# One pair of matmuls moved between two tiles, a one-column read for an order, and one more superblock of partial DMA sums

## The chip, the cores and the metric

The kernel runs on one core of one Trainium2 chip. The metric is the device time of one execution in microseconds. A core has a matmul engine (TensorE, "PE" in the profile, with its weight loads as "PEld"), a vector engine (VectorE, "DVE"), an activation engine (ScalarE, "ACT"), a general engine (GpSimd, "POOL") and a queue engine (SyncE, "SP"). Each works through its own list of instructions in order. They wait for one another by semaphores. Transfers are issued from the SP and POOL lists and land later.

## What is computed

Two operators in a row: a convolution of seven taps whose weights are a softmax that differs for each token and head, and a two-layer network with `h - tanh(h)` between the layers.

```python
def _attn_ref(x, weight_gen):          # x (8, 4096, 192), weight_gen (8, 4096, 8, 7)
    w = np.exp(weight_gen - max)  ;  w = w / (sum(w) + 1e-09)      # over the 7 taps
    x_pad = six rows of zeros ahead of each sequence
    out[b, s, h, g] = sum_k w[b, s, h, k] * x_pad[b, s + k, h, g]  # 8 heads of 24

def _moe_ref(x, w_in, w_out):          # x (32768, 192), w_in (192, 2048), w_out (2048, 192)
    h = x @ w_in
    g = h - np.tanh(h)
    return g @ w_out
```

## The kernel before, in words

**Superblocks.** The 32768 tokens are cut into 32 superblocks of 1024 tokens (`NTOT = 32`), eight tokens per partition. Superblock n goes through four stages, and the loop at L509 runs these stages of different superblocks side by side:

1. *Softmax weights* (ScalarE exp at L145, VectorE sums, reciprocals, scaling at L159 to L198), three superblocks ahead.
2. *Products* (`products`, L204): GpSimd multiplies the seven shifted views of x by their weights, one instruction per tap at L223, into bf16 tiles: taps 0, 2, 4 into `even`, taps 1, 3, 5 into `odd`, tap 6 into `last`. It runs two superblocks ahead. Then the taps must be added up. A DMA issued from GpSimd's list (L240) adds `odd` onto `even`. For superblocks in `PART` (2 to 5) it is issued after tap 3 and adds only the first two pairs of taps; for later ones it is issued after tap 5 and adds nearly all of the three pairs.
3. *Convolution sums* (`conv_sums`, L259): TensorE adds up what is left of the taps and turns the result around by matmuls with an identity, at L276, into PSUM tiles `pc`. A superblock in `PART` has five terms for each of the three channel chunks. A later one has four terms for chunks 0 and 1, five for chunk 2. The sums for superblock n + 1 stand in superblock n's part of TensorE's list: those of chunks 0 and 1 between the matmuls of output block 6 (the first six of its f steps are free of them), then those of chunk 2. Chunks 0 and 1 are copied out by ScalarE (L302), chunk 2 by VectorE (L300), into `convT`.
4. *The network* (`gemm1` L314, `gemm2` L340). The 2048 hidden units are 16 f tiles of 128. `gemm1(n, f)` is six matmuls of 64 rows by 512 columns into a PSUM tile `ph` (L319), then Tanh on ScalarE (`th`, L330), then `ph - th` on VectorE (`gt`, L331). `gemm2(i)` makes the output block i of 128 tokens; there are eight per superblock, each with sixteen f steps (L353). Superblock n's loop makes the blocks of superblock n - 1: after each two f tiles of `gemm1` comes one output block (`out_block`, L506, p = 0 to 7).

**Row halves.** The array is used as two halves of 64 rows that run at the same time: r = 0 and r = 1. In `gemm1` both halves add into the same result. In `gemm2`, half 0 does the first 64 hidden units of each f tile for block i, while half 1 does the other 64 for block i - 1. So a block is finished one `out_block` later, and then ScalarE copies it from its PSUM bank (`obank`, two of them, L372) to `out_sb`. The first matmul of block i writes the bank that block i - 2 has left, so it waits for that copy. For the very first block the second half could overtake the first half in the same bank, since the first has no partner yet. An order written out by hand (L363) makes the second half's first matmul wait for a ScalarE instruction that itself waits for the matmuls before: `g1_act[0]`, the Tanh of the last f tile but one.

**Buffers that matter here.** `ph` and `pc` share three PSUM buffers. So `gemm1(n, 1)` takes the buffer that f tile 14 of superblock n - 1 used, and waits for VectorE's subtraction of that tile. `gt` of each f tile has two buffers.

**The end of a superblock** (L547 to L573): f tiles 12 and 13, block 6 mixed with the convolution sums of chunks 0 and 1, chunk 2, the first two f steps of block 7, f tiles 14 and 15, and the other fourteen f steps of block 7. Then superblock n + 1 begins with f tiles 0 and 1 and its block 0.

The order of instructions is as written in the program (`tc.manual_schedule()`); semaphores are put in by the framework.

Of the kernel before, what the change touches and what calls it, by code (L numbers as in the profile page):

```python
# [8 lines left out]
FP32 = mybir.dt.float32  # L9
BF16 = mybir.dt.bfloat16  # L10

ACT = mybir.ActivationFunctionType
# [4 lines left out]
def kernel(  # L17
# [8 lines left out]
    nc = tc.nc  # L26
# [5 lines left out]
    P = nc.NUM_PARTITIONS  # L32
# [12 lines left out]
    NPAIR = K // 2  # L45
    ACC = NPAIR * J * D - J * R
    PLAIN = (0, 1)
    PART = (2, 3, 4, 5)
    assert S % TOK == 0 and D % R == 0 and H * GC == R and F % P == 0
    assert NFT == 2 * J, "one token block of the second matmul per pair of f tiles"  # L50

    const = ctx.enter_context(tc.tile_pool(name="const", bufs=1))
# [13 lines left out]
    obank = [psum_o.tile([P, 512], FP32, name=f"obank{i}", tag=f"obank{i}") for i in range(2)]  # L66
    zero = const.tile([1, D], FP32, name="zero")
    nc.vector.memzero(zero[:])

    x_of = {}  # L70
    wg_of = {}
# [5 lines left out]
    conv_of = {}  # L77
    g_of = {}
    last_act = {}
    g1_act = {}  # L80
    last_sub = {}
    last_exp = {}
    last_conv = {}
# [2 lines left out]
    def order(inst, other, reason):  # L86
        tc.add_manual_dep(
            inst.ins,
            other.ins.name,
            mybir.DependencyInfo(mybir.DependencyClass.Sync, mybir.DependencyReason.DATA),  # L90
            reason=reason,
        )

    def load_wg(n):
        b, s = divmod(n, NSB)
        s0 = s * TOK
        wg_t = wgpool.tile([P, J, H, K], FP32, name="wg_t")
        nc.sync.dma_start(  # L98
            out=wg_t[:],
            in_=weight_gen[b, s0 : s0 + TOK].rearrange("(p j) h k -> p j h k", p=P),  # L100
        )
        wg_of[n] = wg_t
# [39 lines left out]
    def softmax_exp(n):  # L142
        wg_t = wg_of.pop(n)
        e_t = wgpool.tile([P, J, H, K], FP32, name="e_t")
        last_exp[0] = nc.scalar.activation(  # L145
            out=e_t[:].rearrange("p j h k -> p (j h k)"),
            in_=wg_t[:].rearrange("p j h k -> p (j h k)"),
            func=ACT.Exp,
        )
        e_of[n] = e_t  # L150

    def softmax_tile():
        return wgpool.tile([P, J, H, K], FP32, name="wsm")

    def softmax_sum(n, j0=0, j1=J):

        if j0 == 0:
            zsum_of[n] = wgpool.tile([P, J * H], FP32, name="zsum")
        nc.vector.reduce_sum(  # L159
            out=zsum_of[n][:, j0 * H : j1 * H],  # L160
            in_=e_of[n][:, j0:j1].rearrange("p j h k -> p (j h) k"),
            axis=AX.X,
        )

    def softmax_recip(n, j0=0, j1=J):
        if j0 == 0:
            zr_of[n] = wgpool.tile([P, J * H], FP32, name="zr")
        nc.vector.reciprocal(zr_of[n][:, j0 * H : j1 * H], zsum_of[n][:, j0 * H : j1 * H])  # L168
# [35 lines left out]
    def products(n, taps=None, sums=None, hooks={}, behind=None):  # L204
# [16 lines left out]
        for eng, k, j0, j1 in taps or [(nc.gpsimd, k, 0, J) for k in range(K)]:  # L221
# [12 lines left out]
            if j1 == 1:  # L234
                first_halo[0] = mul
            if (k, n in PART) in ((3, True), (K - 2, False)) and n not in PLAIN:


                acc = 2 * J * D if n in PART else ACC
                nc.gpsimd.dma_start(  # L240
# [8 lines left out]
        if n in PLAIN:  # L249
            prods_of[n] = [[dst[k] for k in (sums or range(K))]] * NC  # L250
        elif n in PART:
            prods_of[n] = [[dst[4], even[:, 0], even[:, 1], dst[5], last[:]]] * NC
# [61 lines left out]
    def gemm1(n, f):  # L314
        convT = conv_of[n]
        ph = psum_h.tile([P, 2, HT], FP32, name="ph", tag="ph")
        for c in range(NC):
            for r in range(2):
                nc.tensor.matmul(  # L319
                    ph[:, r, :],  # L320
                    lhsT=w_in[r * R : (r + 1) * R, c, f * P : (f + 1) * P],
                    rhs=convT[r * R : (r + 1) * R, c, :],
                    start=(c == 0),
                    stop=(c == NC - 1),
                )
        th = tpool.tile([P, TOK], FP32, name="th")
        ph_f = ph[:].rearrange("p r t -> p (r t)")
        g1_act[0] = last_act.get(0)
        gt = gpool.tile([P, TOK], BF16, name=f"gt{f}", tag=f"gt{f}")
        last_act[0] = nc.scalar.activation(out=th[:], in_=ph_f, func=ACT.Tanh)  # L330
        last_sub[0] = nc.vector.tensor_sub(gt[:], ph_f, th[:])  # L331
        g_of.setdefault(n, []).append(gt)

    LAST = (NTOT - 1) * J
    LEAD = 5
    LATE = (1, 2, 3, 4, 5, 6)
    half = {}
    out_of = {}

    def gemm2(i, f0=0, f1=NFT, between=lambda f: None):  # L340

        ops = []
        for r, blk in ((0, i), (1, i - 1)):
            if not 0 <= blk < LAST:
                continue
            n, j = divmod(blk, J)
            if r == 0 and f0 == 0:
                half[blk] = obank[blk % 2]
            ops.append((r, n, j, half[blk]))
        for f in range(f0, f1):  # L350
            for r, n, j, po in ops:
                col = (j % 2) * HT + (j // 2) * P
                mm = nc.tensor.matmul(  # L353
                    po[:, 0:D],
                    lhsT=g_of[n][f][r * R : (r + 1) * R, col : col + P],
                    rhs=w_out[r * R : (r + 1) * R, f, :],
                    start=(r == 0 and f == 0),
                    stop=(r == 1 and f == NFT - 1),
                )
                if r == 1 and f == 0 and i in (1, LAST):  # L360


                    order(mm, g1_act[0] if i == 1 else last_act[0], "row tiles in one bank")  # L363
            between(f)
        if i > 0 and f1 == NFT:
            blk = i - 1
            n, j = divmod(blk, J)
            po = half.pop(blk)
            if j == 0:
                out_of[n] = opool.tile([P, J, D], FP32, name="out_sb")  # L370
            out_sb = out_of[n]
            last_act[0] = nc.scalar.activation(out=out_sb[:, j, :], in_=po[:, 0:D], func=ACT.Copy)  # L372
            if j == J - 1:
                out_of.pop(n)
                g_of.pop(n)
                nc.sync.dma_start(
                    out=out[n * TOK : (n + 1) * TOK, :].rearrange("(p j) e -> p j e", p=P),
                    in_=out_sb[:],
                )
# [126 lines left out]
    def out_block(n, p, f0=0, f1=NFT, between=lambda f: None):  # L506
        gemm2((n - 1) * J + p, f0, f1, between)

    for n in range(1, NTOT):  # L509
        for p in range(J):  # L510
            more = n < NTOT - 1
            if more and p == 6:
                break
            gemm1(n, 2 * p)
            gemm1(n, 2 * p + 1)
            if n == 1:

                if p == 0:
                    load_wg(5)
                if p <= 1:  # L520
                    softmax_sum(3, p * JH, (p + 1) * JH)
                elif p <= 3:
                    softmax_recip(3, (p - 2) * JH, (p - 1) * JH)
                else:
                    softmax_sum(4, (p - 4) * JH, (p - 3) * JH)
                if p == 2:
                    softmax_exp(4)
                if p == 3:
                    wsm_of[3] = (softmax_tile(), None, e_of[3], zr_of[3])
                    products(3)  # L530
            elif n + 3 < NTOT:
                if p == 0:
                    softmax_exp(n + 3)
                if p == 0 and n + 4 < NTOT:
                    load_wg(n + 4)
                if 1 <= p <= 2:
                    softmax_sum(n + 3, (p - 1) * JH, p * JH)
                if 3 <= p <= 4:
                    softmax_recip(n + 3, (p - 3) * JH, (p - 2) * JH)
            out_block(n, p)  # L540
            if p == 0 and 1 < n < NTOT - 2:
                products(n + 2, behind=last_sub[0])
            if p == 0 and n + 3 < NTOT and n not in LATE:
                load_x(n + 3)
        if not more:
            continue
        gemm1(n, 12)  # L547
        gemm1(n, 13)
        if n == 1:
            softmax_recip(4)  # L550

        pcs = []
        sums = conv_sums(n + 1, ((0, 1),), pcs)
        mix = -(-len(prods_of[n + 1][0]) * 2 * 2 * JH // (NFT - LEAD))
        out_block(n, 6, between=lambda f: some(sums, mix if f >= LEAD else 0))
        some(sums, K * 4 * JH)
        conv_out(n + 1, ((0, 1),), pcs)
        pcs = []
        some(conv_sums(n + 1, ((2,),), pcs), K * 4 * JH)


        out_block(n, 7, 0, 2)
        conv_out(n + 1, ((2,),), pcs, nc.vector)
        if n + 3 < NTOT:

            softmax_norm(n + 3, pcs[0][:, 0])
        gemm1(n, 14)
        gemm1(n, 15)
        out_block(n, 7, 2)
        if n in LATE:  # L570


            load_x(n + 3, last_conv[0])  # L573
# [36 lines left out]
```

## Time and profile before

The median of 13 executions is 757.44 us (756.44 to 758.04). The profiled execution took 758.04 us; its span from first to last instruction is 756.2 us.

| | us busy | share of the span | instructions |
|---|---|---|---|
| TensorE matmuls | 734.3 | 97% | 14784 |
| TensorE weight loads | 579.0 | 77% | 14784 |
| VectorE | 695.6 | 92% | 740 |
| ScalarE | 625.1 | 83% | 839 |
| GpSimd | 670.7 | 89% | 264 |

| group | count | mean ns of one |
|---|---|---|
| Tanh, 128x1024 (L330) | 512 | 1022 |
| subtraction, 128x1024 (L331) | 512 | 1219 |
| gemm2 matmul, 64x192 (L353) | 7936 | 243 |
| gemm1 matmul, 64x512 (L319) | 3072 | 378 |
| product of one tap (L223) | 218 | about 3070 |
| copy of an output block (L372) | 248 | 331 |
| accumulating DMA, 1024 KB (L240) | 26 | lands after 8800 |
| accumulating DMA, 768 KB (L240) | 4 | lands after 7600 |

A matmul's length in the profile reaches from its start to a modelled end. Matmuls overlap, so what one costs in a row of many is the distance between starts, and a sum of such rows can call TensorE busy while it waits for a moment. The same distance read between the two halves is a pair's. The granted clock of TensorE is full in all 40 slices of the profile.

### The profile page before, as it was taken

How to read it: one execution, taken by the hardware profiler on the slowest of the kernel's cores; microseconds unless marked ns; L12 is line 12 of the kernel's file. 1: busy time of each engine (PE TensorE's matmuls, PEld its weight loads, DVE VectorE, ACT ScalarE, POOL GpSimd, SP SyncE). 2: the span in 40 equal slices, each digit the busy share in tenths (PEclk: the TensorE clock that was granted, in tenths of full speed). 3: DMA queues.
4: the chain of work that ended last, by engine and by line, in shares of the span. 5: the costliest groups of instructions: out<-in, count | busy, mean ns of one | idle time of the engine just before them, and what ended most of it. 6: DMA issues, size and time to landing. Idle time of an engine off the chain costs nothing.

```text
span 756.2 us, 32326 instructions
## 1 busy us (share of the span) xinstructions
PE 734.3 (97%) x14784; PEld 579.0 (77%) x14784; DVE 695.6 (92%) x740; ACT 625.1 (83%) x839; POOL 670.7 (89%) x264
## 2 busy tenths in 40 slices
PE   3899999999999999999999999999999999999997
PEld 2477778877777877777877787778777777778777
DVE  7989999999999999999999999999999999998893
ACT  3888888788888888888888888888888888888883
POOL 7999999999999999999999999999999999999000
PEclk9999999999999999999999999999999999999999
DMA  8935544566546665554666544666544566542312
GB/s 225 212 80 164 158 149 101 129 184 177 158 138 170 185 183 142 139 139 143 181 186 170 115 132 150 175 180 187 112 130 148 170 185 172 120 113 63 79 45 86
DMA packets 25943, 111.08 MB, mean 147 GB/s; under 512 B 4703, under 2 KB 9551, under 8 KB 21838
## 3 DMA queue, kind: packets, MB, share of 16 engines
q1 hardware_dynamic: 14718, 77.03, 28.4%
q0 software_dynamic: 11088, 31.99, 24.8%
q8 instruction: 115, 1.88, 1.0%
q14 instruction: 22, 0.18, 0.1%
HBM read 54.52 MB, written 25.17 MB: 105 GB/s over the span
## 4 chain that ended last, share of the span: by engine, by line
PE 80%; POOL 17%; DMA 2%; issue 1%; SPq 0%; DVE 0%; ACT 0%; POOLq 0%
PE obank L353 37%; PE ph L319 36%; POOL even L223 7%; POOL odd L223 6%; PE pc L276 5%; POOL last L223 2%; PE po L390 1%; DMA even<-odd 1%; DMA x_t<-in_x_dram 1%; POOL wsm L198 0%; POOL even L240 0%; POOL w_in L432 0%; POOL w_out L419 0%; SPq L98 0%; DVE out_sb L404 0%
## 5 line engine op out<-in xcount | busy, mean ns | idle before, releaser
L331 DVE TENSOR_TENSOR gt<-ph,th 128x1024 bf16<-128x1024 f32 x512 | 602.5, 1219 | 36.0 <-ACT th L330 33.0
L330 ACT ACTIVATE th<-ph 128x1024 f32<-128x1024 f32 x512 | 497.3, 1022 | 72.4 <-PE ph L319 69.5
L353 PE MATMUL obank<-w_out,gt 64*128 64x192 bf16 x7936 | 407.9, 243 | 1.0 <-issue 0.5
L353 PEld LDWEIGHTS <-gt 64*128 64x128 bf16 x7936 | 355.4, 94 | 49.9 <-ACT th L330 0.8
L319 PE MATMUL ph<-convT,w_in 64*128 64x512 bf16 x3072 | 384.6, 378 | 4.7 <-DVE gt L331 2.7
L223 POOL TENSOR_TENSOR even<-x_t,wsm 128x1536 bf16<-128x1536 f32 x93 | 285.2, 3067 | 15.9 <-DVE gt L331 15.5
L223 POOL TENSOR_TENSOR odd<-x_t,wsm 128x1536 bf16<-128x1536 f32 x93 | 284.9, 3064 | 0.0
L319 PEld LDWEIGHTS <-w_in 64*128 64x128 bf16 x3072 | 177.3, 94 | 108.7 <-issue 20.1
L372 ACT ACTIVATE out_sb<-obank 128x192 f32<-128x192 f32 x248 | 82.0, 331 | 36.7 <-PE obank L353 30.0
L223 POOL TENSOR_TENSOR last<-x_t,wsm 128x1536 bf16<-128x1536 f32 x32 | 106.7, 3333 | 0.4 <-DMA x_t<-in_x_dram 0.4
L276 PE MATMUL pc<-ident,even 64*128 64x64 bf16 x2256 | 63.0, 191 | 1.3 <-DMA even<-odd 1.1
L276 PEld LDWEIGHTS <-even 64*128 64x128 bf16 x2304 | 59.9, 96 | 2.4 <-DMA even<-odd 1.2
L240 POOL DMA_DIRECT2D even<-odd x30 | 36.1, 1205 | 9.3 <-POOL odd L223 9.3
L276 PE MATMUL pc<-ident,last 64*128 64x64 bf16 x752 | 27.2, 191 | 9.5 <-POOL last L223 9.5
L302 ACT ACTIVATE convT<-pc 128x1024 bf16<-128x1024 f32 (+1 forms) x33 | 32.7, 993 | 2.4 <-PE pc L276 2.4
L276 PEld LDWEIGHTS <-last 64*128 64x128 bf16 x768 | 23.3, 96 | 9.7 <-POOL last L223 9.5
L159 DVE TENSOR_REDUCE zsum<-e_t 128x32 f32<-128x224 f32 (+1 forms) x61 | 23.7, 388 | 2.9 <-ACT e_t L145 2.9
L300 DVE CAST convT<-pc 128x512 bf16<-128x512 f32 x30 | 20.7, 690 | 4.5 <-PE pc L276 2.9
L145 ACT ACTIVATE e_t<-wg_t 128x448 f32<-128x448 f32 x32 | 18.5, 577 | 7.6 <-DMA wg_t<-in_weight_gen_dram 7.6
L168 DVE RECIPROCAL zr<-zsum 128x32 f32<-128x32 f32 (+1 forms) x58 | 20.3, 350 | 0.0
L198 DVE TENSOR_TENSOR wsm<-e_t,pc 128x448 f32<-128x448 f32 x28 | 17.4, 621 | 2.9
L276 PE MATMUL pc<-ident,odd 64*128 64x64 bf16 x400 | 14.4, 199 | 1.4 <-POOL odd L223 0.8
(28 smaller groups left out, 77.0 us busy)
## 6 DMA issues: line engine op xcount, KB each, us to landing
x_t<-in_x_dram SPq DMA_DIRECT2D x31, 1344.0 KB, 9.3
even<-odd POOLq DMA_DIRECT2D x26, 1024.0 KB, 8.8
out_dram<-out_sb SPq DMA_DIRECT2D x31, 768.0 KB, 7.2
wg_t<-in_weight_gen_dram SPq DMA_DIRECT2D x32, 224.0 KB, 9.7
even<-odd POOLq DMA_DIRECT2D x4, 768.0 KB, 7.6
x_t<-in_x_dram SPq DMA_DIRECT2D x1, 768.0 KB
w_out<-in_moe_w_out_dram POOLq DMA_DIRECT2D x1, 768.0 KB, 9.4
out_dram<-out_sb SPq DMA_DIRECT2D x4, 192.0 KB, 1.9
```

The costliest lines, as they stand in the source:

```text
L159: nc.vector.reduce_sum(out=zsum_of[n][:, j0 * H : j1 * H], in_=e_of[n][:, j0:j1].rearrange("p j h k -> p (j h) k"), axis=AX.X,)
L168: nc.vector.reciprocal(zr_of[n][:, j0 * H : j1 * H], zsum_of[n][:, j0 * H : j1 * H])
L223: mul = eng.tensor_mul(dst[k][:, :, j0:j1].rearrange("p c j h g -> p j h c g"), x_t[:, k + j0 : k + j1, :].rearrange("p j (h c g) -> p j h ...
L240: nc.gpsimd.dma_start(out=even[:].rearrange("p i c j h g -> p (i c j h g)")[:, 0:acc], in_=odd[:].rearrange("p i c j h g -> p (i c j h g)" ...
L276: nc.tensor.matmul(pc[r][:, col : col + R] if home else pc[:, r, col : col + R], lhsT=prods[c][gi][r * R : (r + 1) * R, c, 2 * j : 2 * j + ...
L300: eng.tensor_copy(out, pc[:, :, 0:cols].rearrange("p r (cj t) -> p r cj t", t=R))
L302: last_conv[0] = nc.scalar.activation(out=out, in_=pc[:, :, 0:cols].rearrange("p r (cj t) -> p r cj t", t=R), func=ACT.Copy,)
L319: nc.tensor.matmul(ph[:, r, :], lhsT=w_in[r * R : (r + 1) * R, c, f * P : (f + 1) * P], rhs=convT[r * R : (r + 1) * R, c, :], start=(c == ...
L330: last_act[0] = nc.scalar.activation(out=th[:], in_=ph_f, func=ACT.Tanh)
L331: last_sub[0] = nc.vector.tensor_sub(gt[:], ph_f, th[:])
L353: mm = nc.tensor.matmul(po[:, 0:D], lhsT=g_of[n][f][r * R : (r + 1) * R, col : col + P], rhs=w_out[r * R : (r + 1) * R, f, :], start=(r == ...
L372: last_act[0] = nc.scalar.activation(out=out_sb[:, j, :], in_=po[:, 0:D], func=ACT.Copy)
```

## The change

Three edits in one:

- In superblocks 2 to 31 the first f step of output block 0 (one matmul of each row half) is placed between f tiles 0 and 1 instead of behind f tile 1. The other fifteen f steps stay behind f tile 1. The name `FILL` stands for a 2 that was there before.
- In superblock 1, the second half of the first block waits for a new ScalarE instruction instead of the Tanh of f tile 2: a Copy of one column of `ph` of f tile 2, put just ahead of that Tanh, to a tile `once` that nothing reads.
- Superblock 6 joins `PART`: its accumulating DMA is issued after tap 3 and adds two pairs of taps, and TensorE sums five terms for each chunk.

```diff
-    PART = (2, 3, 4, 5)
+    PART = (2, 3, 4, 5, 6)
...
+    once = const.tile([P, 1], FP32, name="once")
...
-        g1_act[0] = last_act.get(0)
         gt = gpool.tile([P, TOK], BF16, name=f"gt{f}", tag=f"gt{f}")
+        if n == 1 and f == 2:
+
+            probe[0] = nc.scalar.activation(out=once[:], in_=ph_f[:, 0:1], func=ACT.Copy)
         last_act[0] = nc.scalar.activation(out=th[:], in_=ph_f, func=ACT.Tanh)
...
+    FILL, AHEAD = 2, 1
...
-                    order(mm, g1_act[0] if i == 1 else last_act[0], "row tiles in one bank")
+                    order(mm, probe[0] if i == 1 else last_act[0], "row tiles in one bank")
...
             gemm1(n, 2 * p)
+            ahead = AHEAD if p == 0 and n > 1 else 0
+            if ahead:
+                out_block(n, p, 0, ahead)
             gemm1(n, 2 * p + 1)
...
-            out_block(n, p)
+            out_block(n, p, ahead)
...
-        out_block(n, 7, 0, 2)
+        out_block(n, 7, 0, FILL)
...
-        out_block(n, 7, 2)
+        out_block(n, 7, FILL)
```

## The prediction

> **What bounds the kernel now.** I read the chain that ended last first, then TensorE's waits, then superblock lengths, then the timeline at the three places edited.
>
> ```profile
> PE 80%; POOL 17%; DMA 2%; issue 1%; SPq 0%; DVE 0%; ACT 0%; POOLq 0%
> ```
>
> ```profile
> 136.37 2.86 POOL odd L223
> 139.52 9.61 DMA even<-odd
> 151.46 1.36 PE ph L319 x12
> ```
>
> The first is the chain by engine; the second shows three of its pieces in order of time (start, length, what). Until 139.5 us it runs through GpSimd's products, then one accumulating DMA, and after that TensorE to the end. That DMA feeds superblock 6, so TensorE must have stood still for it, and what TensorE lost earlier was hidden by it. Its waits (total, times, longest, in us) agree:
>
> ```profile
> PE ph L319 <- DVE gt L331: 2.7, 8, 0.5
> PE pc L276 <- DMA even<-odd: 1.1, 1, 1.1
> ...
> PE obank L353 <- ACT th L330: 0.4, 1, 0.4
> ```
>
> The eight DVE waits lie in the start-up before 30 us, which the change leaves alone. Lengths of superblocks 5, 4 and 11 (window, length, busy time by engine), cut where the first gemm1 matmul starts:
>
> ```profile
> 130.00:153.79 23.79, 22.74 (x462) 19.52 (x460) 21.39 (x24) 19.38 (x27) 23.49 (x10) 1.00 0.54 146
> 107.22:130.00 22.78, 22.78 (x477) 18.15 (x473) 21.42 (x24) 19.38 (x27) 22.48 (x9) 1.00 0.48 143
> 267.01:289.57 22.56, 22.56 (x461) 17.77 (x458) 21.42 (x24) 19.31 (x27) 22.26 (x9) 1.00 0.56 156
> ```
>
> Superblock 11 shows TensorE "busy" all of 22.56 us at full clock. The starts of single matmuls show its pace: a gemm1 pair (both row halves) every 0.2155 us, so 0.65 per f tile; a gemm2 pair every 0.0825; a convolution pair every 0.029. 16 x 0.65 + 128 x 0.0825 + 52 x 0.029 = 22.4. So 0.1 us or so per superblock is lost, and it hides inside rows that call themselves busy:
>
> ```profile
> 309.66 1.50 PE L319 MATMUL ph<-convT,w_in 64*128 64x512 bf16 x12
> ...
> 310.53 1.94 ACT L330 ACTIVATE th<-ph 128x1024 f32<-128x1024 f32 x2 [0.24 <-PE ph L319]
> ...
> 310.98 1.33 PE L353 MATMUL obank<-w_out,gt 64*128 64x192 bf16 x28
> 311.58 4.83 DVE L331 TENSOR_TENSOR gt<-ph,th 128x1024 bf16<-128x1024 f32 x4 [0.22 <-ACT th L330]
> ...
> 312.14 1.55 PE L319 MATMUL ph<-convT,w_in 64*128 64x512 bf16 x12
> 312.35 0.33 ACT L372 ACTIVATE out_sb<-obank 128x192 f32<-128x192 f32 x1
> ...
> 314.82 1.48 PE L319 MATMUL ph<-convT,w_in 64*128 64x512 bf16 x12
> ```
>
> The twelve matmuls of f tiles 0 and 1 of superblock 13 (312.14) take 1.55 us, any later twelve (314.82) 1.48. The 0.07 is a wait: f tile 1 takes the PSUM buffer of f tile 14, which the DVE subtraction gives back. That chain is gemm1 of f 14 to 310.31, Tanh 310.53 to 311.55, subtraction 311.58 to 312.81, then 0.05 to TensorE: 312.86. TensorE's own work in between (f 14, 15, fourteen pairs of block 7, f 0) ends at 312.78.
>
> **Part A, the output block that begins early (superblocks 2 to 31).** One gemm2 pair moves from behind f tile 1 to ahead of it: two weight loads, two matmuls, no DMA; no other queue sees it. TensorE's work inside the loop grows from 2.455 to 2.54 us against a latency of 2.53, so the wait goes and nothing is added. The wait, by the starts of single matmuls, is 0.047 to 0.102 us in superblocks 7 to 31, together 1.93 us; at most 0.0825 can be covered each time, which leaves 0.06 of it in superblocks 7, 14 and 30: **gain 1.87 us**. Superblocks 2 to 5 show at most 0.002 us here, since their wait (0.107 us) falls at f tile 15, on ScalarE's convT copy; the early pair costs nothing there and gains nothing. After the wait goes, f tile 3 is next: it now has 0.13 us of slack behind the subtraction of f 0, and keeps 0.06.
>
> The moved pair brings its own wait ahead of f tile 1: its bank must have been copied out (the 0.33 us row at 312.35). The copy ends at 312.687; ScalarE's release reaches TensorE some 0.05 us later (the convT copy ended at 128.154 and its waiter started at 128.206), so 312.74 against the pair's slot at 312.784: cover 0.04 us, in superblocks 7, 14 and 30 0.02. Queued behind a late pair would be f tile 1, Tanh, subtraction, everything. The built program has this matmul wait for the copy and nothing later, as before.
>
> A rule speaks against this part. The Trainium skill, "TensorE: Matmul & The Clock Gate", Single matmul latency, prices a lone matmul with its drain unhidden at (398 + N)/2.4 ns: 248 ns for N = 192, an estimate from that page. The row of these matmuls has a mean of 243 ns. If a pair set between two f tiles cost that, f tile 1 would start 0.17 us later than now and only 0.08 would come back behind it: 25 times 0.09, and 0.17 in each of superblocks 2 to 6, so 3.1 us lost instead of 1.87 gained. But the trace has such a short run already: block 7's first two pairs, between convolution and f 14, run from 127.290 to the next gemm1 matmul at 127.454, 0.082 each. I take 0.082; the drain is under the next matmuls.
>
> **Part B, the ScalarE read (superblock 1, once).**
>
> ```profile
> 41.71 1.94 ACT L330 ACTIVATE th<-ph 128x1024 f32<-128x1024 f32 x2 [0.66 <-PE ph L319]
> ...
> 42.15 0.24 PE L353 MATMUL obank<-w_out,gt 64*128 64x192 bf16 x1
> ...
> 42.79 1.49 PE L353 MATMUL obank<-w_out,gt 64*128 64x192 bf16 x31 [0.39 <-ACT th L330]
> ```
>
> Block 1's second row half waits for the whole Tanh of f tile 2 (41.71 to 42.74). The next first-half matmul started at 42.794 instead of 42.236: 0.56 us lost. The read starts at the same 41.71. Its length no row shows. The rows of 192 and 1024 elements (331 and 1022 ns) put it on 172 ns + 0.83 per element: 0.17 us; the ceiling is the 331 row. It ends at 41.88 to 42.04, plus 0.05: before 42.10 either way, so the wait goes whole. The Tanh behind it starts 0.07 to 0.25 later (consecutive ScalarE rows overlap by 0.1), and with it the subtraction of f 2, which f tile 5 needs: slack 0.64 - 0.56 - delay gives a new wait of 0 to 0.17. I take 0.04: **gain 0.52 us**, 0.39 to 0.56.
>
> **Part C, partial sums in superblock 6.** GpSimd issues its accumulating DMA after product 3 instead of 5, two products (5.7 us) earlier, and 768 KB instead of 1024; the issue takes the same 1.5 us out of GpSimd's queue, so product 6 and all of superblock 7 keep their times. Landing goes from 149.1 to 141 or 142 (133.8 plus the 6.7 to 8.3 us of the four like it); needed from 147.9. Product 6 ends at 143.7, needed past 148. TensorE's wait there is 1.244 us from start to start, 1.22 over the usual. Against it: 16 more matmuls, 8 pairs x 0.029 = 0.23; and f 15 then waits 0.107 as in superblock 4 instead of 0.065, while f tile 1 of superblock 6 loses its 0.045. **Gain 0.99**; the lengths of superblocks 5 and 4 say 23.79 - 22.78 = 1.01.
>
> B counts only because C takes out the wait that would swallow it. What is late next: superblock 7's DMA landed at 169.89, needed at 171.71; TensorE comes 1.5 us sooner, leaving 0.2. Superblock 11's landed at 260.18, needed at 262.40, now at 260.5: 0.3. Others have 0.9 or more. GpSimd's last product for superblock 2 ended at 56.34, needed at 57.88 - 0.5.
>
> **The sum.** 1.87 + 0.52 + 0.99 = 3.4 us. The profiled execution took 758.04 (span 756.2), so 754.7 there; from the median of 757.44, **754.1**.
>
> **Rivals.** *The next DMA takes it back.* Superblocks 7 and 11 have 0.2 and 0.3 us of cover, and such landings spread from 6.7 to 12.9 us. For it: TensorE moves against a GpSimd that doesn't. Against: stores and loads behind TensorE move earlier too, and superblock 8 has 1.5 us. It gives back 0.3 to 1.2: 754.4 to 755.3.
>
> *A gains nothing*: the copy's release comes 0.075 us behind the slot and the wait only changes its name. For it: 0.04 us of cover. Then 757.44 - 1.5 = 755.9.
>
> *Slower: the moved pair waits on ScalarE.* Place: first matmul of each superblock's block 0, 30 times. It loses per superblock what the release is later than 0.075 past the slot; the whole kernel is slower by over 1.5 us from 0.175 on, a release 0.22 us later than now. If it stood behind the Tanh of f 0 (313.00 to 314.03) it would be 1.22 us x 30: about 792. Against it: in the trace the same matmul starts at 313.506, before that Tanh ends.
>
> **How the numbers follow.** Forecast as summed, 753.0 to 754.9: 0.70 (the lower end if the four TensorE stalls that the profile lays to nothing, 1.2 us in all, shrink; they may also grow). DMA takes back: 0.12. A empty: 0.09. Slower: 0.05. The rest, small shifts of code or data, 0.04. No change means within 0.2%, 1.5 us, about what a measurement tells. The first two are faster, and half of A empty; so faster 0.86, same 0.08, slower 0.06. Range 753.0 to 755.6.
>
> **What would show it.** Right: superblock 5 at 22.8 us and no wait on the DMA; superblock 11 at 22.48; no gap at 42.15; a tiny Copy row of some 0.2 us. Wrong: the first gemm2 pair of a superblock starting later than 0.65 us after its f tile 0; a new DMA wait near 170 or 260; or superblocks still at 22.56.

## The result and the profile after

The changed kernel takes **754.05 us** in the median of 10 runs (753.53 to 755.57), beside 757.42 before; the ratio is 0.9957, 95% interval 0.9949 to 0.9964. The forecast was 754.1. The same kernel measured once more, below, took 754.54, so part of the close agreement is luck. The profiled execution took 754.10 us with a span of 752.3.

TensorE's waits in the changed kernel (who waited for whom, total, times, longest, in us). Its line numbers are a few higher than before: L320 is gemm1's matmul, L358 gemm2's, L333 the Tanh, L332 the new read.

```profile
PE pc L277 <- POOL last L224: 9.3, 1, 9.3
PE ph L320 <- DVE gt L334: 2.4, 8, 0.3
...
PE pc L277 <- issue: 0.6, 1, 0.6
PE pc L277 <- DMA even<-odd: 0.5, 1, 0.5
```

The wait of `obank` for a Tanh is gone. A DMA wait is still listed, but it is another one. The superblock lengths tell which. Superblocks 5, 4, 11, 7 and 8, cut as before (window, length, busy time of each engine):

```profile
128.77:151.56 22.79, 22.79 (x478) 18.04 (x475) 21.43 (x24) 19.39 (x27) 22.49 (x10) 1.00 0.50 144
105.99:128.77 22.78, 22.78 (x477) 18.02 (x474) 21.43 (x24) 19.39 (x27) 22.48 (x9) 1.00 0.47 138
265.38:287.87 22.49, 22.49 (x461) 17.81 (x458) 21.42 (x24) 19.31 (x27) 22.19 (x9) 1.00 0.57 156
174.05:197.22 23.17, 22.67 (x461) 17.86 (x458) 21.46 (x24) 19.34 (x27) 22.87 (x9) 1.00 0.70 211
197.22:220.39 23.17, 22.61 (x462) 17.85 (x458) 21.38 (x24) 19.30 (x27) 22.87 (x10) 1.00 0.55 151
```

Superblock 5 has fallen from 23.79 to 22.78 and superblock 11 from 22.56 to 22.49, as forecast. Superblock 7 holds the remaining DMA wait, superblock 8 a stop of TensorE that no semaphore explains ("issue"); the last section comes back to it.

The place where superblock 13 begins, TensorE alone, in the timeline:

```profile
309.21 1.33 PE L358 MATMUL obank<-w_out,gt 64*128 64x192 bf16 x28
310.36 0.83 PE L320 MATMUL ph<-convT,w_in 64*128 64x512 bf16 x6
311.01 0.26 PE L358 MATMUL obank<-w_out,gt 64*128 64x192 bf16 x2
311.09 0.83 PE L320 MATMUL ph<-convT,w_in 64*128 64x512 bf16 x6
311.74 1.42 PE L358 MATMUL obank<-w_out,gt 64*128 64x192 bf16 x30
```

The row of twelve has become six, the early pair, and six. The pair starts 0.65 us behind f tile 0, so without a wait of its own. f tile 1 follows 0.08 later and takes 0.65 to the next pair. The row of the pair says 0.26 us; what it costs is the 0.08 between starts.

Superblock 1, all engines, around the new read:

```profile
41.12 0.17 ACT L332 ACTIVATE once<-ph 128x1 f32<-128x1 f32 x1 [0.67 <-PE ph L320]
41.18 1.94 ACT L333 ACTIVATE th<-ph 128x1024 f32<-128x1024 f32 x2
41.34 1.47 PEld L358 LDWEIGHTS <-gt 64*128 64x128 bf16 x32
41.51 1.53 PE L358 MATMUL obank<-w_out,gt 64*128 64x192 bf16 x32
```

All 32 matmuls of block 1 now stand in one row. The read took 171 ns and held the Tanh up by 0.07 us.

Where the 3.9 us between the two spans (756.24 and 752.33) went:

| piece | before | after | difference | what it is |
|---|---|---|---|---|
| start to superblock 1 | 38.19 | 37.59 | -0.60 | start-up, 37.7 to 40.2 in the other profiles |
| superblock 1 | 23.47 | 22.83 | -0.64 | the read (B) |
| superblocks 2 to 4 | 68.35 | 68.35 | 0.00 | |
| superblock 5 | 23.78 | 22.78 | -1.00 | the DMA wait (C) |
| superblock 6 | 22.68 | 22.49 | -0.19 | a wait at f tile 1 and a stop in the convolution |
| superblocks 7 and 8 | 45.42 | 46.34 | +0.93 | a DMA wait and a stop without a semaphore, against the early pair's gain |
| superblocks 9 to 30 | 497.18 | 494.85 | -2.33 | the early pair (22 x 0.07) and stops of 0.8 in before |
| from superblock 31 | 37.17 | 37.09 | -0.08 | the early pair |

The accounts of single executions hold about one microsecond of chance on each side. The steady lengths (median of superblocks 9 to 30: 22.563 before, 22.493 after) don't.

### The profile page after: what moved, and what is told of

It reads as the page before. It is cut to its first block, busy times and chain, and to the rows that moved or that the text cites. A ratio compares the mean times of both kernels' runs of the same rounds, so it can differ in the third digit from the quotient of the medians.

```text
span 752.3 us, 32359 instructions
## 1 busy us (share of the span) xinstructions
PE 732.0 (97%) x14800; PEld 576.5 (77%) x14800; DVE 695.5 (92%) x740; ACT 625.0 (83%) x840; POOL 670.6 (89%) x264
## 4 chain that ended last, share of the span: by engine, by line
PE 74%; POOL 22%; DMA 2%; issue 2%; SPq 0%; DVE 0%; ACT 0%; POOLq 0%
PE obank L358 34%; PE ph L320 33%; POOL even L224 9%; POOL odd L224 9%; PE pc L277 5%; POOL last L224 3%; PE po L395 1%; DMA even<-odd 1%; DMA x_t<-in_x_dram 1%; POOL wsm L199 0%; POOL even L241 0%; POOL w_in L437 0%; POOL w_out L424 0%; SPq L99 0%; DVE out_sb L409 0%
## 5 line engine op out<-in xcount | busy, mean ns | idle before, releaser
L333 ACT ACTIVATE th<-ph 128x1024 f32<-128x1024 f32 x512 | 497.3, 1022 | 69.8 <-PE ph L320 68.4
L358 PE MATMUL obank<-w_out,gt 64*128 64x192 bf16 x7936 | 411.9, 243 | 0.0
L358 PEld LDWEIGHTS <-gt 64*128 64x128 bf16 x7936 | 355.9, 94 | 56.2
L320 PE MATMUL ph<-convT,w_in 64*128 64x512 bf16 x3072 | 384.4, 378 | 4.4 <-DVE gt L334 2.4
L320 PEld LDWEIGHTS <-w_in 64*128 64x128 bf16 x3072 | 173.7, 94 | 101.7 <-issue 12.9
```

The costliest lines, as they stand in the source:

```text
L320: nc.tensor.matmul(ph[:, r, :], lhsT=w_in[r * R : (r + 1) * R, c, f * P : (f + 1) * P], rhs=convT[r * R : (r + 1) * R, c, :], start=(c == ...
L358: mm = nc.tensor.matmul(po[:, 0:D], lhsT=g_of[n][f][r * R : (r + 1) * R, col : col + P], rhs=w_out[r * R : (r + 1) * R, f, :], start=(r == ...
```

## The experiments

The ratios are to the median of before in the same session (757.38 for the first four rows, 757.49 for "again", "one pair from block 7" and "wide read", 757.40 for the rest). The last four columns are lengths of single superblocks in each kernel's profile, in us.

| kernel | us | ratio, 95% interval | superblock 1 | 4 | 5 | 12 |
|---|---|---|---|---|---|---|
| A alone | 755.22 | 0.9970 (0.9959 to 0.9981) | 23.47 | 22.78 | 23.91 | 22.49 |
| B alone | 757.04 | 0.9995 (0.9987 to 1.0003) | 22.83 | 22.78 | 24.03 | 22.56 |
| C alone | 756.48 | 0.9992 (0.9985 to 0.9998) | 23.47 | 23.04 | 22.96 | 22.56 |
| B and C | 755.73 | 0.9982 (0.9973 to 0.9990) | 22.83 | 22.78 | 22.82 | 22.56 |
| all three, again | 754.54 | 0.9960 (0.9947 to 0.9974) | 22.83 | 22.78 | 22.78 | 22.49 |
| two pairs ahead | 754.68 | 0.9967 (0.9954 to 0.9980) | 22.83 | 22.78 | 22.78 | 22.54 |
| three and three | 754.83 | 0.9966 (0.9955 to 0.9978) | 22.74 | 23.02 | 22.94 | 22.54 |
| one pair from block 7 | 756.31 | 0.9987 (0.9980 to 0.9994) | 22.91 | 22.87 | 22.87 | 22.57 |
| superblock 8 in PART | 754.83 | 0.9962 (0.9949 to 0.9975) | 22.83 | 22.79 | 22.78 | 22.49 |
| pair held by a Tanh | 792.18 | one run | 22.83 | 24.08 | 24.08 | 23.83 |
| wide read | 754.06 | one run | 23.25 | 22.83 | 22.96 | 22.49 |

### The three parts one by one

A alone keeps the early pair and takes back the other two edits:

```diff
-    PART = (2, 3, 4, 5, 6)
+    PART = (2, 3, 4, 5)
...
-        if n == 1 and f == 2:
-            probe[0] = nc.scalar.activation(out=once[:], in_=ph_f[:, 0:1], func=ACT.Copy)
+        g1_act[0] = last_act.get(0)
...
-                    order(mm, probe[0] if i == 1 else last_act[0], "row tiles in one bank")
+                    order(mm, g1_act[0] if i == 1 else last_act[0], "row tiles in one bank")
```

> The early gemm2 pair alone, with the Tanh order and the old PART. My theory: the pair fills TensorE's wait ahead of f tile 1, so superblocks 9 to 31 take 22.49 us instead of 22.56, and the kernel is 1.7 to 1.9 us faster than before (about 755.6); the 1.0 us wait for superblock 6's DMA and the gap at 42 us stay. Rival (the pair costs the full length of a lone matmul): 3 us slower. Rival (the gain of the whole change lies in the other two parts): no change.

It is 2.2 us faster than before by the medians, with 1.4 to 3.1 in the interval. The lone-matmul rival falls. Superblocks 5 and 12:

```profile
132.05:155.96 23.91, 22.73 (x463) 19.38 (x459) 21.39 (x24) 19.39 (x27) 23.61 (x10) 1.00 0.54 147
291.45:313.94 22.49, 22.49 (x462) 17.79 (x458) 21.42 (x24) 19.32 (x27) 22.02 (x9) 1.00 0.57 156
```

All undisturbed superblocks are at 22.49, and the waits of the other parts stand: 23.47 in superblock 1, 23.91 in superblock 5.

B alone sets `AHEAD = 0` and takes superblock 6 out of PART:

```diff
-    PART = (2, 3, 4, 5, 6)
+    PART = (2, 3, 4, 5)
...
-    FILL, AHEAD = 2, 1
+    FILL, AHEAD = 2, 0
```

> The one-column read alone, without the early pair and with the old PART. My theory: TensorE gains 0.5 to 0.65 us in superblock 1, but then waits as much longer for superblock 6's DMA (1.6 to 1.9 us from start to start instead of 1.24), so the time is that of before within 0.2 us. Rival (the parts simply add up): 0.5 to 0.65 us faster.

Superblock 1 gains its 0.64 us, and superblock 5 grows to 24.03. The time is that of before within its interval. TensorE's step at the DMA wait is 1.41 us instead of 1.24; I had named 1.6 to 1.9. Of the 0.47 that is missing, 0.14 is start-up, which put TensorE later against GpSimd in this execution, and 0.25 is the DMA, which landed in 9.36 us instead of 9.61; some 0.08 stays open. The swallowing shows without such corrections: from the landing of superblock 6's DMA to the end of the span it is 607.1 us in both (756.24 - 149.13 before, 755.48 - 148.35 here).

C alone has the old Tanh order, `AHEAD = 0`, and superblock 6 in PART:

```diff
-        if n == 1 and f == 2:
-            probe[0] = nc.scalar.activation(out=once[:], in_=ph_f[:, 0:1], func=ACT.Copy)
+        g1_act[0] = last_act.get(0)
...
-    FILL, AHEAD = 2, 1
+    FILL, AHEAD = 2, 0
...
-                    order(mm, probe[0] if i == 1 else last_act[0], "row tiles in one bank")
+                    order(mm, g1_act[0] if i == 1 else last_act[0], "row tiles in one bank")
```

> Superblock 6 in PART alone, with the Tanh order and without the early pair. My theory: superblock 5 shortens from 23.79 to 22.78 us, and the kernel is 0.8 to 1.1 us faster (about 756.5), unless a later DMA takes some of it back. Rival (the 16 extra matmuls and the later convT copy cost what the wait did): no change.

0.90 us faster by the medians (0.15 to 1.1 by the interval), and no DMA wait is left in its profile. Superblock 5 took 22.96 rather than 22.78 here, and superblocks 4 and 8 were longer too: TensorE stopped there for 0.1 to 0.7 us with no wait that explains it.

B and C is the changed kernel with `AHEAD = 0`.

> The changed kernel without the early pair (AHEAD = 0). My theory: B counts now because C took out the wait that swallowed it: 1.5 to 1.65 us faster than before (about 755.9), so 0.6 us faster than C alone, although B alone gives nothing; superblocks 9 to 31 are at 22.56 us. Rival (B is worth nothing at all): as C alone.

1.65 us faster by the medians, 0.75 more than C alone, while B alone gave nothing that can be told from zero. The intervals of the two kernels overlap, so the medians alone don't settle B. The profiles do: superblock 1 takes 22.83 instead of 23.47, and no DMA wait follows that could take the 0.64 back. So B's gain is real and was hidden by C's wait. The early pair adds the rest, 755.73 to 754.05. Superblock 11 without it:

```profile
265.23:287.79 22.56, 22.56 (x461) 17.79 (x458) 21.42 (x24) 19.33 (x27) 22.26 (x9) 1.00 0.56 156
```

With it, the steady superblocks take 22.49.

### Is the wait of the early pair really absent?

```diff
+                if r == 0 and f == 0 and f1 == 1:
+                    order(mm, last_act[0], "late")
```

> The changed kernel with the early pair's first matmul made to wait for the Tanh of f tile 0 as well, to price the wait of my slower rival and to show that it is not there in the changed kernel. My theory: the pair starts about 1.3 us past its slot in each of 30 superblocks, each superblock takes 22.49 + 1.3 = 23.7 to 23.8 us, and the kernel takes 754 + 30 x 1.3, 790 to 794 us. If other engines can take up part of such a delay: well below 785.

792.18 us. TensorE's waits in this kernel begin with:

```profile
PE obank L358 <- ACT th L333: 33.5, 30, 1.1
```

Thirty waits, one in each superblock, and a steady superblock of 23.79: 1.30 longer, hardly any of it taken up elsewhere. This is the price that the slower rival named (about 792), and it shows that the changed kernel doesn't pay it.

### Is it the wait that the pair fills, or the moving?

Two pairs ahead of f tile 1:

```diff
-    FILL, AHEAD = 2, 1
+    FILL, AHEAD = 2, 2
```

> The changed kernel with two f steps of block 0 ahead of f tile 1 instead of one (AHEAD = 2). My theory: the wait ahead of f tile 1 is already gone (it was at most 0.1 us, the pair is 0.083), so the second pair only changes places: the same time within 0.2 us as the changed kernel. If the pair gained by something else than that wait (each pair moved is worth 0.07 us per superblock): 1.7 us faster again. If a moved pair has a cost of its own: slower.

22.49 again in steady superblocks (the median of 9 to 30), and a time of 754.68 whose interval covers the changed kernel's. The second pair is worth nothing, so it is the wait and not the moving.

One pair into the same loop, but from block 7:

```diff
-    FILL, AHEAD = 2, 1
+    FILL, AHEAD = 1, 0
```

> The changed kernel with the extra pair in the loop taken from the other side: FILL = 1 and AHEAD = 0, so one pair of block 7 moves from ahead of f tile 14 to behind f tile 15, and block 0 stays whole. My theory: the wait ahead of f tile 1 goes here too, since only the work between f 14 and f 1 counts, but f tile 15's wait for the convT copy grows by the same pair (0.03 to 0.11 us, and 0.107 to 0.19 in superblocks 1 to 5): superblocks 9 to 31 stay at 22.54 to 22.57 us, superblocks 2 to 5 grow to 22.86, and the time is 1.6 to 2.2 us above the changed kernel. Rival (any pair put into the loop gains): 22.49 us and the time of the changed kernel.

As expected in time: 22.87 in superblocks 2 to 5, 22.57 in 9 to 30, and 756.31 us. Superblocks 3 and 11:

```profile
83.84:106.71 22.87, 22.86 (x478) 18.05 (x474) 21.43 (x24) 19.43 (x27) 22.57 (x10) 1.00 0.49 141
265.77:288.34 22.57, 22.57 (x461) 17.72 (x458) 21.42 (x24) 19.39 (x27) 22.27 (x9) 1.00 0.57 156
```

f tile 1 no longer waits (it starts 0.648 us behind f tile 0 in superblock 13, against 0.724 before), but something else does. In superblocks 1 to 5 it is f tile 15, on the convT copy: 0.19 us instead of 0.107. In the steady ones I had named the same place, and that was wrong. There f tile 14 itself starts later: 0.178 us after the last pair of block 7 instead of 0.095, just as the subtraction of f tile 13 ends. The pair that leaves was covering that wait.

Three and three:

```diff
-    FILL, AHEAD = 2, 1
+    FILL, AHEAD = 3, 3
```

> The changed kernel with three f steps of block 7 ahead of f tile 14 (FILL = 3) and three of block 0 ahead of f tile 1 (AHEAD = 3). My theory: the second wait of a superblock, f tile 15 on ScalarE's convT copy (0.03 us in most superblocks, 0.107 in 1 to 5), is covered by the third pair of block 7, and the loop from f tile 14 to f tile 1 keeps its length because block 0 gives it two more: 22.46 us in superblocks 9 to 31, 22.70 in 2 to 5, and 0.8 to 1.2 us faster than the changed kernel. Rival (the bank copy of block 6 then ends too late for the early pair, whose cover is 0.04 us): no gain.

No gain; the rival named for it holds. Superblock 13's start in this kernel, first TensorE, then ScalarE:

```profile
310.43 0.83 PE L320 MATMUL ph<-convT,w_in 64*128 64x512 bf16 x6
311.14 0.42 PE L358 MATMUL obank<-w_out,gt 64*128 64x192 bf16 x6
...
310.75 0.34 ACT L377 ACTIVATE out_sb<-obank 128x192 f32<-128x192 f32 x1
```

The early pairs start at 311.14, 0.71 behind f tile 0 instead of 0.65: the copy of the bank (310.75 to 311.09) is now what they wait for. ScalarE works through two Tanh and then the copy without a stop, so the copy keeps its time against f tile 14 while TensorE comes 0.11 sooner. The waits at f tiles 14 and 15 are gone, and 0.06 of the gain is paid back here.

### How short must the read be?

```diff
-    once = const.tile([P, 1], FP32, name="once")
+    once = const.tile([P, 512], FP32, name="once")
...
-            probe[0] = nc.scalar.activation(out=once[:], in_=ph_f[:, 0:1], func=ACT.Copy)
+            probe[0] = nc.scalar.activation(out=once[:], in_=ph_f[:, 0:512], func=ACT.Copy)
```

> The changed kernel with the read made 512 columns wide instead of one. It should take 0.6 us instead of 0.171. My theory: only the read's end counts, against a slot 0.39 us after its start; so 0.2 to 0.3 us of the wait come back, and as the Tanh behind it starts 0.5 us late, up to 0.3 more at f tile 5: superblock 1 takes 23.05 to 23.45 us instead of 22.83, less than the 23.47 of before. Rival (the gain came from waiting on another instruction at all, or from the order in the row halves, not from the read's shortness): 22.83.

Superblock 1 takes 23.25 us, in the expected 23.05 to 23.45. The timeline of this kernel:

```profile
41.31 0.60 ACT L332 ACTIVATE once<-ph 128x512 f32<-128x512 f32 x1 [0.66 <-PE ph L320]
...
41.96 1.27 PEld L358 LDWEIGHTS <-gt 64*128 64x128 bf16 x31 [0.33 <-ACT once L332]
```

The weight load that waits for the read starts 0.05 us behind its end (41.909). So B's gain goes with the length of the instruction waited for. Of the 0.42 us that come back, 0.19 are lost here and 0.23 at f tile 5, which waits for the subtraction behind the delayed Tanh (44.08, f tile 5 at 44.14). (The total of this single run says nothing here; other pieces of it were lucky.)

### Does the change bring about the new DMA wait?

In the changed kernel's profile, TensorE's step into superblock 8's sums was 0.69 us:

```profile
191.87 0.24 PE L277 MATMUL pc<-ident,last 64*128 64x64 bf16 x4
192.60 0.20 PE L277 MATMUL pc<-ident,even 64*128 64x64 bf16 x2 [0.50 <-DMA even<-odd]
```

The same kernel once more:

> The changed kernel once more, for a second profile. In the first, TensorE waited 0.66 us in superblock 7 for superblock 8's DMA, which took 10.3 us to land. My theory: that landing was late by chance (8.6 to 9.2 us in the variants with the same order), so superblock 7 is 22.5 to 22.6 us this time and there is no DMA wait; the median is again 754.0 within 0.4. Rival (the change brings the wait about, since TensorE now comes sooner): the wait is there again, 0.3 us or more.

No DMA wait is in the second profile; that DMA was issued at 182.61 and landed at 191.39, in 8.78 us instead of 10.33. In the six variants that keep its order and TensorE's pace it took 8.63 to 8.89. So it was one late landing; what made it late, no run shows. The median of 754.54 (754.07 to 754.68) is 0.5 above the first, a little outside the 0.4 that I had allowed. Superblocks 7 and 8 took 22.89 and 23.44 here, with stops laid to "issue".

Superblock 8 in PART as well:

```diff
-    PART = (2, 3, 4, 5, 6)
+    PART = (2, 3, 4, 5, 6, 8)
```

> The changed kernel with superblock 8 in PART too. In its profile TensorE waited 0.66 us for superblock 8's DMA (landed 192.56). My theory: that wait goes, for 0.23 us of extra matmuls and about 0.08 more wait at f tile 15, so 0.3 us faster in an execution like the profiled one. Rival (the wait stands in few executions and the profiled one had bad luck): 0 to 0.3 us slower. Either way the DMA of superblock 8 is issued 5.7 us earlier and no wait for it is left.

The DMA was issued at 176.41 and landed at 186.48, five microseconds ahead of its use, and superblock 7 took 22.78: 0.29 more than the 22.49 of an undisturbed one. At 754.83 the median is not below the changed kernel's, and its interval covers it. By the times alone the two can't be told apart. The wait that the cover guards against stood in one of two profiles of the changed kernel and in none of those six variants, while the cover costs its 0.29 each time. No variant beat the changed kernel.

## Why the prediction was right, and where its terms were off

**What bounds the kernel.** The TensorE reading held: B alone is swallowed, C frees it, and the sum of the three is met (3.4 us forecast, 3.37 by the medians). That it is met so closely is partly luck: A came out 0.12 below its term and B 0.12 above, and the second measurement of the same kernel gave 2.95.

**Part A**, forecast 1.87 us: 25 superblocks of 0.070 (22.563 less 22.493) are 1.75. The wait itself was sized rightly; the pair is a little longer than the wait, so f tile 1 starts 0.006 us later behind f tile 0 than before (0.730 against 0.724), which the sum left out. By the medians A is worth 2.2 alone and 1.7 on top of B and C. The pair's price of 0.08 us is shown by the starts at 311.01 and 311.09; the estimate for a lone matmul comes to 0.246 for N = 192, not the 0.248 of the forecast. Its cover of 0.04 against the bank copy held in the steady superblocks, and was used up at once when "three and three" brought TensorE 0.11 sooner.

**Part B**, forecast 0.52 us, measured 0.64 in superblock 1. The estimate of the read, 0.17 us from two longer rows, was met at 0.171. Two terms were mis-sized. The loss was read off one row half alone (0.56). From the last two matmuls of f tile 3 to the first two of f tile 4, one of each half, it was 0.62 for the earlier of the two and 0.65 for the later. And the new wait at f tile 5 came, 0.04 us for its first matmul (43.517, behind a subtraction that ended at 43.458), but the half that was behind started on time (43.525), so it cost nothing.

**Part C**, forecast 0.99, measured 1.00. The landing came at 140.67: before the "141 or 142" of the text, within the 140.5 to 142.1 of its own sum.

**What was late next.** Superblocks 7 and 11, named with 0.2 and 0.3 us of cover (for 7, the forecast's own figures leave 0.3), were in time: DMAs landed at 168.59 and 257.60, needed at 169.43 and 260.76. For superblock 7 that was a fast landing, 7.92 us; with the 8.82 of before it would have come 0.06 late. The one that came late in the first profile was superblock 8's, which had been given 1.5 us. It took 10.33 us where before it took 8.72: the spread of the landings, not their mean, decided. The rival as a standing loss is refuted by the second profile. The stops without a semaphore, which the forecast let shrink or grow, moved instead (last section).

**The slower rival** was priced rightly, and is absent.

## What to carry to other kernels

When one engine is "busy" for all of a loop's length, work out its time from start-to-start distances; what is left over is waits of under 0.1 us that the wait list here did not show, and in a loop of 32 they added up to nearly two microseconds. To fill such a wait, try work from behind it before work from ahead of it: ahead there can be another wait that this work was covering, as in "one pair from block 7". And a gain that comes before a later wait on a slower engine counts only when that wait is gone, so parts of a change have to be tried together as well as alone.

## What the runs showed of the hardware that was not expected

The two row halves of the array drift apart when one has less to do. Before the change, in superblock 1:

```profile
40.62 0.39 PE L319 MATMUL ph<-convT,w_in 64*128 64x512 bf16 x1
40.78 0.24 PE L353 MATMUL obank<-w_out,gt 64*128 64x192 bf16 x1
40.84 1.47 PE L319 MATMUL ph<-convT,w_in 64*128 64x512 bf16 x11
```

A gemm1 matmul of one half starts (40.62) while gemm2 matmuls that stand ahead of it in the list are still being started in the other half (40.78). The Trainium skill, "TensorE: Matmul & The Clock Gate", The mechanism, says that matmuls start and end strictly in program order; across row halves this trace differs for the starts, and it is what the order by hand guards against.

TensorE also stops now and then with no semaphore to explain it. From superblock 1 on, the twelve profiles other than that of "pair held by a Tanh" have twenty such stops of over 0.32 us from start to start, the longest 1.02. All nine profiles with superblock 6 in PART and the usual pace have one of 0.45 to 1.0 us in superblock 8, at 216 to 217 us. The three with the old PART have none there; theirs is at 194 to 197 us, and two of them have another near 332.

The traces tell what these places have in common. Count TensorE's weight loads and matmuls through from the first, in order of their starts, and cut the row into blocks of 256: each of the twenty stops stands just ahead of the 194th instruction of a block. The waits that have a semaphore stand at other counts. And the profile's list of DMA queues has one of the same grain (packets, MB, share of 16 engines):

```profile
q8 instruction: 115, 1.88, 1.0%
```

These are 115 packets of 16 KB, beside 29600 weight loads and matmuls in the changed kernel: one for about every 256 of them. Each of the twenty stops ends 1.2 to 1.55 us after such a packet has ended. This speaks strongly for TensorE waiting for the next block of its own instructions; no run was made to test it. It fits the places too: part C adds 16 matmuls and 16 weight loads to the list, so another stretch of it lies at the border of a block. With the start-up, these stops make up much of the difference between single profiles.
